# Key and value pooling and two engines' part of the weight conversion, emitted between a chunk's logarithm and its last three steps

## The chip, the cores and the metric

The kernel runs on one core of one Trainium2 chip. The metric is the device time of one execution in microseconds. Five queues run beside each other on the core: TensorE (PE, with its weight loads as PEld), VectorE (DVE), ScalarE (ACT), GpSimd (POOL) and SyncE (SP), which here issues every DMA.

## The reference

Three layers in a row: attention over pooled keys and values, a feed-forward layer with a rational activation, and a gated layer. The five weight matrices are float64, which the kernel reads as pairs of int32; the other inputs are float32.

```python
k_p = k.reshape(B, H, Sp, 8, D).mean(axis=3)      # B 8, H 8, S 576, D 64
v_p = v.reshape(B, H, Sp, 8, D).mean(axis=3)
scores = 1 / sqrt(D) * q @ k_p.transpose(0, 1, 3, 2)
attn = softmax(scores)
x = (attn @ v_p)                                  # 4608 tokens x 512
h = x @ w_in                                      # 512 x 2048
P = a[0] + a[1]*h + a[2]*h**2 + a[3]*h**3
Q = 1 + abs(b[0])*abs(h) + abs(b[1])*h**2
x = (P / (Q + 1e-6)) @ w_out                      # 2048 x 512
out = (sigmoid(x @ w_gate) * (x @ w_val)) @ w_out2
```

## The kernel before

**Chunks.** The feed-forward layer goes over 9 blocks of 512 tokens and, in each, over 16 slices of 128 hidden features: 144 chunks, counted by `n`. For each chunk the loop (L753 to L787) emits: `g1`, 12 matmuls into one of four PSUM banks tagged "h"; attention pieces for TensorE; `rational1` (three activations L509 to L511 on ScalarE, then L512 to L514 on VectorE, the polynomials); attention pieces that go first; `split_g` of the chunk before (L494 on ScalarE, L497 on GpSimd); `rational2` (the logarithm L520 and the exponential L522, which make the reciprocal in the chunk's own PSUM bank); `rational3` (L526 to L528 on VectorE); `g2` of the chunk three back, 12 matmuls into four accumulators; then the other attention pieces, and weights. Every engine works its queue in the order of emission.

**Attention.** A tile of up to 128 tokens goes through `scores` (matmuls L343; maximum and subtraction L354, L356 on VectorE), `exponential` (L362), `normalise` (L369 to L372 on VectorE, L373 on GpSimd), `a_transpose` and `attend`, whose end is L404 and L405. For each of 8 batches, five pieces of the keys are pooled by VectorE (L302) and five of the values by GpSimd (L319, L320). All are Python generators. A table `plan` gives each its step and a rank; `run(on_pe, n, part)` resumes each generator of the chunk once, for what it does on TensorE, and `run(off_pe, n, part)` resumes it a second time, for the rest. Part 0 goes ahead of `split_g`, part 1 behind `g2`. Pooling and its like have nothing on TensorE: `ew` (L408) yields at the first resumption and works at the second. The order of `plan` within a step also sets the order in which the pieces are loaded, three ahead.

**Weights.** A float64 matrix arrives as pairs of int32. `conv1` makes one float32 of each pair: L90 and L92 on ScalarE, L94 (a shift) and L96 (a mask and an or) on VectorE, L98 (an addition) on GpSimd. `conv2` splits it into a high and a low part: L102 on ScalarE, L103 on GpSimd. In chunks 0 to 15, `weights_a` converts a slice of `w_in` and one of `w_out` at each chunk's end, `conv1` two chunks ahead of `conv2`. From chunk 16 to chunk 111, `background` prepares the gated layer's weights in 12 units of 8 chunks: three loads, `conv1` at chunks 2, 3 and 6 of a unit, four subtractions L199 on GpSimd at chunk 4, splits by `bg_split` (L175 on ScalarE, L176 on GpSimd, a store L177 from one of two buffers) at chunks 5 to 7, and `conv2` at chunk 7 into the buffer whose store was issued at chunk 6.

Behind the chunks comes the gated layer, which TensorE fills.

Of the kernel before, what the change touches and what calls it, by code (L numbers as in the profile page):

```python
# [11 lines left out]
I32 = mybir.dt.int32  # L12
# [23 lines left out]
def attention_moe_glu_kernel(ctx: ExitStack, tc: tile.TileContext, q, k, v, w_in, w_out, ca, cb, w_gate, w_val, w_out2, out):  # L36
# [14 lines left out]
    NCH = (H * SP + P - 1) // P  # L51
# [24 lines left out]
    def new_tmp(name, tag="m", bufs=3):  # L76
        return rot.tile([P, 512], F32, tag=tag, name=name, bufs=bufs)
# [3 lines left out]

    def conv1(*raws):

        ws = [(raw[:, :, 1], raw[:, :, 0], new_tmp("wx").bitcast(I32)[:, :raw.shape[1]]) for raw in raws]
        for hw, lw, x in ws:


            nc.scalar.activation(hw.bitcast(F32), hw.bitcast(F32), AF.Copy, scale=2.0 ** -112)  # L90

            nc.scalar.activation(lw, lw.bitcast(U32), AF.Copy, scale=2.0 ** -29)  # L92
        for hw, lw, x in ws:
            nc.vector.tensor_scalar(out=x, in0=hw, scalar1=3, scalar2=None, op0=ALU.logical_shift_left)  # L94
        for hw, lw, x in ws:
            nc.vector.scalar_tensor_tensor(out=hw, in0=hw, scalar=-2 ** 31, in1=x, op0=ALU.bitwise_and, op1=ALU.bitwise_or)  # L96
        for hw, lw, x in ws:
            nc.gpsimd.tensor_tensor(out=hw, in0=hw, in1=lw, op=ALU.add)  # L98

    def conv2(raw, wh, wl, eng=nc.gpsimd):  # L100
        t = raw[:, :, 1].bitcast(F32)
        nc.scalar.activation(wh, t, AF.Copy)  # L102
        eng.tensor_tensor(out=wl, in0=t, in1=wh.bitcast(F32), op=ALU.subtract)  # L103
# [27 lines left out]
    def wi_conv1(f):  # L131
        conv1(wi_raw[f])
# [81 lines left out]
    with tc.manual_schedule():  # L214
# [29 lines left out]
        units, raws, loaded = [], {}, [0]  # L244
# [12 lines left out]
        def load_unit(start=False, tag=None):  # L257
            if loaded[0] == len(units):
                return
            u = units[loaded[0]]  # L260
            loaded[0] += 1
            if tag:
                t = tag[0].tile([P, 4 * P], F32, tag=tag[1], name="raw1")
            elif start:
                t = early([P, 4 * P], "raw0")
            else:
                t = raw_p.tile([P, 4 * P], F32, tag="raw", name="raw")
            if u[0] == "q":
                b, t0, n = tiles[u[1]]
                o = (b * S + t0) * H * D  # L270
                nc.sync.dma_start(t[:, :NJ * n], q[o:o + n * H * D].rearrange("(p x) -> p x", p=P))
            elif u[0] == "k":
                cols = k_cols(u[2])
                nc.sync.dma_start(t[:, :(cols.stop - cols.start) * POOL], k[u[1], :, cols.start * POOL:cols.stop * POOL])
            else:
                rows = v[u[1]].rearrange("h (s j) d -> (h s) (j d)", j=POOL)
                c = u[2]
                m = P if c < NCH - 1 else CL
                nc.sync.dma_start(t[:m], rows[c * P:c * P + m])
            raws[u] = t  # L280
            if not start and not tag:
                in_ring.add(u)
# [142 lines left out]
        plan = []  # L425
        n0 = len(of_block[0])

        def put(step, rank, pe, rest, gen, *a, use=()):
            plan.append((step, rank, len(plan), pe, rest, gen(*a), use))
# [17 lines left out]
        for b in range(1, B):  # L447
            e0, e1 = max(at[first[b - 1]], -2), at[last[b - 1]]
            for c in range(2 * NCH):
                w, f = (("k", pool_k), ("v", pool_v))[c // NCH]  # L450
                put(e0 + c * (e1 - 3 - e0) // (2 * NCH), 6, 1, 1, ew, f, b, c % NCH, use=[(w, b, c % NCH)])
            put(e1 - 2, 3.5, 1, 1, ew, place_k, b)
            put(e1 + (e1 > NF1), 1, 0, 0, ew, mask_v, b)
        plan.sort(key=lambda x: (x[0], x[4], x[1], x[2]))
        units += [u for x in plan for u in x[6]]
        lead = plan[0][0]
        on_pe, off_pe = {}, {}
# [4 lines left out]
        def run(which, step, part):  # L462
            for gen in which.get((step, part), []):
                next(gen, None)
# [37 lines left out]
        def g1(n):  # L502
            i, f = divmod(n, NF1)
            ys[n] = hidden(wi[f], xs[i])

        def rational1(n):
            h = ys[n]
            s, u, y = new_tmp("s", "su", 3), new_tmp("u", "su", 3), new_tmp("y", "y", 3)
            nc.scalar.activation(s, h, AF.Square)  # L509
            nc.scalar.activation(u, h, AF.Abs, scale=coef[:, 4:5])  # L510
            nc.scalar.activation(y, h, AF.Identity, scale=coef[:, 3:4], bias=coef[:, 2:3])  # L511
            nc.vector.scalar_tensor_tensor(out=u, in0=s, scalar=coef[:, 5:6], in1=u, op0=ALU.mult, op1=ALU.add)  # L512
            nc.vector.tensor_tensor(out=y, in0=h, in1=y, op=ALU.mult)
            nc.vector.scalar_tensor_tensor(out=y, in0=y, scalar=coef[:, 1:2], in1=h, op0=ALU.add, op1=ALU.mult)  # L514
            ys[n] = (h, s, u, y)

        def rational2(n):

            h, s, u, y = ys[n]
            nc.scalar.activation(s, u, AF.Ln, scale=2.0 ** LSH, bias=ONE * 2.0 ** LSH)  # L520

            nc.scalar.activation(h, s, AF.Exp, scale=-1.0, bias=LSH * math.log(2.0))  # L522

        def rational3(n):
            r, s, u, y = ys[n]
            nc.vector.scalar_tensor_tensor(out=u, in0=u, scalar=ONE, in1=r, op0=ALU.add, op1=ALU.mult)  # L526
            nc.vector.scalar_tensor_tensor(out=y, in0=y, scalar=coef[:, 0:1], in1=r, op0=ALU.add, op1=ALU.mult)  # L527
            nc.vector.scalar_tensor_tensor(out=y, in0=u, scalar=-2.0, in1=y, op0=ALU.add, op1=ALU.mult)  # L528

        def split_g(n):  # L530
            y = ys.pop(n)[3]
            gs[n] = g = g_p.tile([P, 2, TB], F32R, tag="g", name="g")
            split_hi(g, y)
            split_lo(g, y, nc.gpsimd)

        def g2(n):
            i, f = divmod(n, NF1)
            if f == 0:
                new_acc(i)
            g, wt = gs.pop(n), wo[f]  # L540
            for e in range(NJ):
                es = slice(e * P, (e + 1) * P)
                mm3(acc[i][e], wt[:, 1, es], wt[:, 0, es], g[:, 1], g[:, 0], f == 0, f == NF1 - 1)

        def g2_out(n):
            i, f = divmod(n, NF1)
            if f == NF1 - 1:
                for e in range(NJ):
                    store(acc[i][e], x2d[i][:, e], e < 2, *(("su", 3) if e == NJ - 1 else ()))
# [182 lines left out]
        def weights_a(p):  # L732

            for ahead, f, n in ((3, wi_conv2, NF1), (0, wo_conv2, NF1), (5, wi_conv1, NF1), (2, wo_conv1, NF1),
                                (8, wi_load, NF1), (5, wo_load, NF1)):
                if 0 <= p + ahead < n:
                    f(p + ahead)

        for st in range(lead, 0):
            run(on_pe, st, 0)  # L740
            run(on_pe, st, 1)
            run(off_pe, st, 0)
            run(off_pe, st, 1)
            if st == lead + 1:

                for x in range(NCH):
                    load_unit(tag=later[4 + x])
            weights_a(st)

        nc.scalar.activation(coef[:, 0:4], pc[:, 0:4], AF.Copy, scale=-1.0)  # L750
        nc.scalar.activation(coef[:, 4:6], pc[:, 4:6], AF.Abs)

        for n in range(N1):  # L753
            m = n - LAG
            if n == N1 - NF1:
                att.close()
                late = ctx.enter_context(tc.tile_pool(name="late", bufs=1))
            g1(n)
            run(on_pe, n, 0)
            rational1(n)  # L760
            run(off_pe, n, 0)
            if n >= 1:
                split_g(n - 1)
            rational2(n)
            rational3(n)
            if m >= 0:
                g2(m)
                g2_out(m)
            run(on_pe, n, 1)
            run(off_pe, n, 1)  # L770
            if n < NF1:
                weights_a(n)
            elif n % NF1 >= FS:
                wo_stream(n % NF1)
            background(n - NF1)
            x = n - (N1 - NF1)
            if x == 0:
                rawx = [xs_p.tile([P, 8 * TB], F32, tag="xs", name="rawx")]
                x_load(0)
            if 1 <= x <= NQ:  # L780
                ring_load(x - 1)
            if 3 <= x <= 6:
                x_prep(x - 3)
            if x in (4, 5):
                wo2_load(NF1 - NQ + x - 4)
            if x >= 7:
                wo2_load(x - 7)  # L787
# [68 lines left out]
```

## Time and profile before

| | |
|---|---|
| time, median of 3 runs | 1920.32 us (1919.8 to 1921.81) |
| the profiled execution | 1921.36 us, of which the span is 1919.5 us |
| TensorE busy | 1810.9 us, 94% |
| VectorE busy | 1223.6 us, 64% |
| ScalarE busy | 939.7 us, 49% |
| GpSimd busy | 899.5 us, 47% |
| chain that ended last | TensorE 58%, VectorE 24%, ScalarE 8%, issue 6%, DMA 2%, GpSimd 2% |

Busy shares are means over stages with different limits, so they are read by stretch. A group of instructions is named by its line in the kernel. Of an instruction the timeline gives the start, the time it took, and in brackets how long its engine had stood idle before it and what ended that. An instruction that stands still after it has been started, because something it needs on the way is taken, shows as one that takes longer, and not as a wait.

### The profile page before, as it was taken

What the parts mean: (1) busy time and instruction counts of PE and PEld (TensorE: products, weight loads), DVE (VectorE), ACT (ScalarE), POOL (GpSimd) and SP (SyncE); (2) the same over time, 40 slices, a digit from 0 to 9 for tenths busy, and PEclk for the clock granted to TensorE, in tenths of its full rate; (3) what the DMA queues carried; (4) which work ended last, traced back from release to release, by engine and by line L of the source; (5) the groups of instructions that cost most, each with busy time, mean ns of one, the idle gap of its engine ahead of it and who ended that gap; (6) DMA issues with size and microseconds to landing.
All of it is one profiled execution on the core that took longest, in us unless ns stands there. A gap on an engine that the chain in (4) does not pass through costs nothing.

```text
span 1919.5 us, 25166 instructions
## 1 busy us (share of the span) xinstructions
PE 1810.9 (94%) x8936; PEld 1565.9 (82%) x8936; DVE 1223.6 (64%) x1847; ACT 939.7 (49%) x1754; POOL 899.5 (47%) x855
## 2 busy tenths in 40 slices
PE   5588999999999999999999999999999999999999
PEld 4366777787777778777887899899999998998997
DVE  7999888889888888888778634334243333333331
ACT  4677767677666676766666522322222222222221
POOL 6668556665564665654224233424334335225231
PEclk9788999999999999999999999999999999999999
DMA  6343355344453444353135566465474573663661
GB/s 244 129 151 110 113 183 188 109 179 149 166 175 137 171 148 166 123 193 136 44 118 196 192 225 198 137 216 174 145 239 143 176 231 121 207 213 124 203 198 44
DMA packets 123118, 312.56 MB, mean 163 GB/s; under 512 B 11505, under 2 KB 43249, under 8 KB 122993
## 3 DMA queue, kind: packets, MB, share of 16 engines
q1 hardware_dynamic: 122992, 310.95, 48.1%
q8 instruction: 71, 1.16, 0.2%
q14 instruction: 55, 0.44, 0.1%
HBM read 257.95 MB, written 52.95 MB: 162 GB/s over the span
## 4 chain that ended last, share of the span: by engine, by line
PE 58%; DVE 24%; ACT 8%; issue 6%; DMA 2%; POOL 2%; SPq 0%; ACTq 0%; POOLq 0%; DVEq 0%
PE h L469 12%; PE h L471 11%; PE h L470 11%; DVE u L512 3%; DVE y L514 3%; DVE y L528 3%; DVE u L526 3%; DVE y L527 3%; ACT h L522 3%; PE accA L706 3%; PE accA L707 3%; PE h L707 3%; PE accA L705 3%; PE h L706 3%; PE h L705 3%
## 5 line engine op out<-in xcount | busy, mean ns | idle before, releaser
L642 DVE TENSOR_TENSOR t<-h,t 128x384 f32<-128x384 f32 x360 | 200.7, 558 | 388.3 <-ACT t L650 278.8
L695 POOL TENSOR_TENSOR t<-t 128x384 f32<-128x384 f32 x72 | 84.4, 1172 | 450.3 <-issue 255.0
L497 POOL TENSOR_TENSOR g<-y,g 128x512 fp32r<-128x512 f32 x144 | 189.1, 1313 | 207.5 <-ACT g L494 172.3
L469 PE MATMUL h<-xs,wi 128*128 128x512 f32 x576 | 234.3, 407 | 11.8 <-DVE xs L405 4.5
L469 PE MATMUL acc<-g,wo 128*128 128x512 f32 x576 | 233.1, 405 | 2.2 <-ACT g L494 2.2
L471 PE MATMUL h<-xs,wi 128*128 128x512 f32 x576 | 229.3, 398 | 3.0 <-DVE xs L405 3.0
L470 PE MATMUL h<-xs,wi 128*128 128x512 f32 x576 | 229.4, 398 | 0.0
L471 PE MATMUL acc<-g,wo 128*128 128x512 f32 x576 | 226.4, 393 | 2.4 <-POOL g L497 2.4
L470 PE MATMUL acc<-g,wo 128*128 128x512 f32 x576 | 225.4, 391 | 0.0
L471 PE MATMUL h<-xS,wq 128*128 128x384 f32 x576 | 193.0, 335 | 0.0
L469 PE MATMUL h<-xS,wq 128*128 128x384 f32 x576 | 192.8, 335 | 0.0
L470 PE MATMUL h<-xS,wq 128*128 128x384 f32 x576 | 192.7, 335 | 0.0
L512 DVE SCALAR_TENSOR_TENSOR u<-s,coef,u 128x512 f32<-128x512 f32 x144 | 133.9, 930 | 41.1 <-ACT u L510 40.8
L526 DVE SCALAR_TENSOR_TENSOR u<-u,h 128x512 f32<-128x512 f32 x144 | 99.0, 688 | 92.4 <-ACT h L522 90.6
L469 PE MATMUL h<-xA,wq 128*128 128x384 f32 x432 | 149.2, 345 | 0.0
L471 PE MATMUL h<-xA,wq 128*128 128x384 f32 x432 | 144.7, 335 | 0.0
L470 PE MATMUL h<-xA,wq 128*128 128x384 f32 x432 | 144.6, 335 | 0.0
L469 PEld LDWEIGHTS h<-xs,wi 128*128 128x128 f32 x576 | 111.1, 193 | 39.3 <-DVE xs L405 6.0
L528 DVE SCALAR_TENSOR_TENSOR y<-u,y 128x512 f32<-128x512 f32 x144 | 131.6, 914 | 4.9
L471 PEld LDWEIGHTS h<-xs,wi 128*128 128x128 f32 x576 | 111.2, 193 | 27.9 <-DVE xs L405 3.5
L520 ACT ACTIVATE s<-u 128x512 f32<-128x512 f32 x144 | 91.0, 632 | 87.6 <-DVE u L512 86.1
L469 PEld LDWEIGHTS acc<-g,wo 128*128 128x128 f32 x576 | 108.8, 189 | 28.1 <-ACT g L494 2.6
(122 smaller groups left out, 4290.9 us busy)
## 6 DMA issues: line engine op xcount, KB each, us to landing
wq<-w2d SPq DMA_DIRECT2D x252, 512.0 KB, 4.3
wo<-wod SPq DMA_DIRECT2D x88, 512.0 KB, 4.0
w2d<-wq SPq DMA_DIRECT2D x36, 512.0 KB, 2.9
x2d<-o SPq DMA_DIRECT2D x36, 256.0 KB, 2.3
out_dram<-o SPq DMA_DIRECT2D x36, 256.0 KB, 2.0
raw<-in_k_dram SPq DMA_DIRECT2D x32, 256.0 KB, 2.7
raw<-in_q_dram SPq DMA_DIRECT2D x32, 256.0 KB, 2.7
raw<-in_v_dram SPq DMA_DIRECT2D x32, 256.0 KB, 2.7
```

What stands on the lines that cost most here:

```text
L469: nc.tensor.matmul(out_, wl, xh, start=start, stop=False, skip_group_check=on)
L470: nc.tensor.matmul(out_, wh, xh, start=False, stop=False, skip_group_check=on)
L471: nc.tensor.matmul(out_, wh, xl, start=False, stop=stop, skip_group_check=on)
L497: eng.tensor_tensor(out=g[:, 1], in0=y, in1=g[:, 0].bitcast(F32), op=ALU.subtract)
L512: nc.vector.scalar_tensor_tensor(out=u, in0=s, scalar=coef[:, 5:6], in1=u, op0=ALU.mult, op1=ALU.add)
L520: nc.scalar.activation(s, u, AF.Ln, scale=2.0 ** LSH, bias=ONE * 2.0 ** LSH)
L526: nc.vector.scalar_tensor_tensor(out=u, in0=u, scalar=ONE, in1=r, op0=ALU.add, op1=ALU.mult)
L528: nc.vector.scalar_tensor_tensor(out=y, in0=u, scalar=-2.0, in1=y, op0=ALU.add, op1=ALU.mult)
L642: nc.vector.tensor_tensor(out=out_, in0=a, in1=b, op=ALU.add)
L705: nc.tensor.matmul(a[t], gh, wt[:, 0], start=(f == 0), stop=False)
L706: nc.tensor.matmul(a[t], gh, wt[:, 1], start=False, stop=False)
L707: nc.tensor.matmul(a[t], gl, wt[:, 0], start=False, stop=(f == NF2 - 1))
```

## The change

`conv1` is cut in two. Its activations (`conv1a`) stay where `conv1` was; its VectorE and GpSimd part (`conv1b`) is kept in a list and emitted by `gap()`, between `rational2` and `rational3` of the next chunk. For the pooling pieces the table's entry for the second resumption becomes part 2, which is run in the same place; the entry for the first stays part 1. In `plan`, they are sorted ahead of the other pieces of a step.

```diff
+    def conv1b(*raws):
         ws = [(raw[:, :, 1], raw[:, :, 0], new_tmp("wx").bitcast(I32)[:, :raw.shape[1]]) for raw in raws]
...
+    between = []
+
+    def conv1(*raws):
+        conv1a(*raws)
+        between.append(lambda: conv1b(*raws))
+
+    def gap():
+        for f in between:
+            f()
+        between.clear()
...
-                put(e0 + c * (e1 - 3 - e0) // (2 * NCH), 6, 1, 1, ew, f, b, c % NCH, use=[(w, b, c % NCH)])
+                st = e0 + c * (e1 - 3 - e0) // (2 * NCH)
+                put(st, 6, 1, 1 if st < 0 else 2, ew, f, b, c % NCH, use=[(w, b, c % NCH)])
...
-        plan.sort(key=lambda x: (x[0], x[4], x[1], x[2]))
+        plan.sort(key=lambda x: (x[0], (0, 2, 1)[x[4]], x[1], x[2]))
...
             weights_a(st)
+            gap()
...
             rational2(n)
+            run(off_pe, n, 2)
+            gap()
             rational3(n)
```

**VectorE, end of chunk 1 and start of chunk 2, before.** L94 and L96 are the conversion of a tile of `w_in` (`wiraw`) and one of `w_out` (`woraw`), L369 to L372 the normalisation of chunk 1.

```order
L514 SCALAR_TENSOR_TENSOR y<-y,coef,h 128x512
L526 SCALAR_TENSOR_TENSOR u<-u,h 128x512
L527 SCALAR_TENSOR_TENSOR y<-y,coef,h 128x512
L528 SCALAR_TENSOR_TENSOR y<-u,y 128x512
L369 TENSOR_REDUCE r<-e 64x8
L371 TENSOR_SCALAR r<-r 128x8
L372 RECIPROCAL r<-r 128x8
L94 TENSOR_SCALAR wx<-wiraw 128x512
L96 SCALAR_TENSOR_TENSOR wiraw<-wiraw,wx 128x512
L94 TENSOR_SCALAR wx<-woraw 128x512
L96 SCALAR_TENSOR_TENSOR woraw<-woraw,wx 128x512
L512 SCALAR_TENSOR_TENSOR u<-s,coef,u 128x512
```

And of the change, the same place; L98 and L100 are now the conversion's two lines, L528 to L530 the first three steps, L542 to L544 the last three, L384 to L387 the normalisation.

```order
L530 SCALAR_TENSOR_TENSOR y<-y,coef,h 128x512
L98 TENSOR_SCALAR wx<-wiraw 128x512
L100 SCALAR_TENSOR_TENSOR wiraw<-wiraw,wx 128x512
L98 TENSOR_SCALAR wx<-woraw 128x512
L100 SCALAR_TENSOR_TENSOR woraw<-woraw,wx 128x512
L542 SCALAR_TENSOR_TENSOR u<-u,h 128x512
L543 SCALAR_TENSOR_TENSOR y<-y,coef,h 128x512
L544 SCALAR_TENSOR_TENSOR y<-u,y 128x512
L384 TENSOR_REDUCE r<-e 64x8
L386 TENSOR_SCALAR r<-r 128x8
L387 RECIPROCAL r<-r 128x8
L528 SCALAR_TENSOR_TENSOR u<-s,coef,u 128x512
```

The conversion of chunk 0's tiles, emitted in chunk 0 before, stands in chunk 1 now, between the chunk's first three steps and its last three; chunk 1's own follows in chunk 2.

**GpSimd, chunks 21 to 23 (5 to 7 of a unit), before.** L497 is a chunk's low part, L373 a tile's normalisation, L98 the end of `conv1`, L176 and L103 low parts of split weights.

```order
L497 TENSOR_TENSOR g<-y,g 128x512
L373 TENSOR_TENSOR e<-e,r 128x576
L98 TENSOR_TENSOR wqraw<-wqraw 128x512
L176 TENSOR_TENSOR wq<-wqraw,wq 128x256
L176 TENSOR_TENSOR wq<-wqt,wq 128x256
L497 TENSOR_TENSOR g<-y,g 128x512
L176 TENSOR_TENSOR wq<-wqraw,wq 128x256
L103 TENSOR_TENSOR wq<-wqraw,wq 128x512
```

And of the change, where L513, L388, L102, L191 and L118 are the same in that order.

```order
L513 TENSOR_TENSOR g<-y,g 128x512
L388 TENSOR_TENSOR e<-e,r 128x576
L191 TENSOR_TENSOR wq<-wqraw,wq 128x256
L191 TENSOR_TENSOR wq<-wqt,wq 128x256
L513 TENSOR_TENSOR g<-y,g 128x512
L102 TENSOR_TENSOR wqraw<-wqraw 128x512
L191 TENSOR_TENSOR wq<-wqraw,wq 128x256
L118 TENSOR_TENSOR wq<-wqraw,wq 128x512
```

The end of `conv1` goes behind two splits and the next chunk's low part.

**VectorE, the end of chunk 7, before.** L302 is a pooled piece of the keys, L354 and L356 the softmax's maximum and subtraction.

```order
L528 SCALAR_TENSOR_TENSOR y<-u,y 128x512
L354 TENSOR_REDUCE mx<-sc 128x4 x2
L356 TENSOR_TENSOR e<-sc,mx 128x288 x2
L302 TENSOR_REDUCE kp<-raw 128x64
L94 TENSOR_SCALAR wx<-wiraw 128x512
```

And of the change, where L544, L317, L369 and L371 are the same.

```order
L544 SCALAR_TENSOR_TENSOR y<-u,y 128x512
L317 TENSOR_REDUCE kp<-raw 128x64
L369 TENSOR_REDUCE mx<-sc 128x4 x2
L371 TENSOR_TENSOR e<-sc,mx 128x288 x2
```

The piece stays behind the chunk's last step, and goes ahead of the softmax.

## Rows read from the trace of the kernel before

**Rows 1.** Busy time by stretch (chunks 0 to 15, 16 to 111): stretch, its length, engines.
```profile
core 0: us, PE busy (x) PEld busy (x) DVE busy (x) ACT busy (x) POOL busy (x), PEclk, DMA share, GB/s
45.90:208.70 162.80, 118.16 (x521) 95.04 (x518) 149.52 (x199) 110.94 (x202) 116.22 (x104) 0.84 0.37 127
208.70:886.10 677.40, 642.70 (x3085) 523.96 (x3086) 581.76 (x902) 467.32 (x875) 398.22 (x410) 0.99 0.45 157
```

**Rows 2.** Waits of VectorE, 46 to 209 us: total, times, longest.
```profile
DVE u L526 <- ACT h L522: 10.6, 14, 1.0
```

**Rows 3.** Waits of VectorE and of ScalarE, 209 to 886 us.
```profile
DVE u L526 <- ACT h L522: 57.8, 84, 1.0
...
ACT wq L102 <- DMA w2d<-wq: 29.3, 12, 3.3
```

**Rows 4.** Timeline of VectorE, chunks 1 and 2: start, time, instruction, [idle before].
```profile
60.67 0.74 DVE L512 SCALAR_TENSOR_TENSOR u<-s,coef,u 128x512 f32<-128x512 f32 x1
...
63.82 0.69 DVE L526 SCALAR_TENSOR_TENSOR u<-u,h 128x512 f32<-128x512 f32 x1 [1.03 <-ACT h L522]
...
66.90 0.39 DVE L94 TENSOR_SCALAR wx<-wiraw 128x512 int32<-128x512 int32 x1
67.32 4.03 DVE L96 SCALAR_TENSOR_TENSOR wiraw<-wiraw,wx 128x512 int32<-128x512 int32 x1
...
77.28 1.48 DVE L528 SCALAR_TENSOR_TENSOR y<-u,y 128x512 f32<-128x512 f32 x1
...
80.14 0.40 DVE L94 TENSOR_SCALAR wx<-wiraw 128x512 int32<-128x512 int32 x1
...
82.98 0.74 DVE L512 SCALAR_TENSOR_TENSOR u<-s,coef,u 128x512 f32<-128x512 f32 x1
```

**Rows 5.** Timeline of GpSimd, the same chunks.
```profile
67.06 1.23 POOL L373 TENSOR_TENSOR e<-e,r 64x576 f32<-64x576 f32 x1 [3.52 <-DVE r L372]
...
69.51 1.29 POOL L103 TENSOR_TENSOR wo<-woraw,wo 128x512 fp32r<-128x512 f32 x1
...
78.17 1.76 POOL L103 TENSOR_TENSOR wo<-woraw,wo 128x512 fp32r<-128x512 f32 x1
```

**Rows 6.** Group of the large key pieces, 0 to 900 us: busy us, mean ns.
```profile
L302 DVE TENSOR_REDUCE kp<-raw 128x64 f32<-128x512 f32 x32 | 21.0, 668 | 3.2 <-DMA raw<-in_k_dram 3.2
```

**Rows 7.** Timeline of ScalarE, chunk 2.
```profile
75.27 0.60 ACT L522 ACTIVATE h<-s 128x512 f32<-128x512 f32 x1 [0.81 <-DVE y L514]
```

**Rows 8.** Timelines of VectorE and of GpSimd, end of chunk 13.
```profile
192.33 1.52 DVE L94 TENSOR_SCALAR wx<-woraw 128x512 int32<-128x512 int32 x1
...
194.91 0.95 DVE L512 SCALAR_TENSOR_TENSOR u<-s,coef,u 128x512 f32<-128x512 f32 x1
...
191.82 1.74 POOL L497 TENSOR_TENSOR g<-y,g 128x512 fp32r<-128x512 f32 x1
```

**Rows 9.** Timelines and, with the DMA, the chain that ended last, chunks 22 and 23.
```profile
255.38 0.69 DVE L96 SCALAR_TENSOR_TENSOR wqraw<-wqraw,wx 128x512 int32<-128x512 int32 x1
...
263.48 0.83 DVE L512 SCALAR_TENSOR_TENSOR u<-s,coef,u 128x512 f32<-128x512 f32 x1 [1.96 <-ACT u L510]
...
256.20 1.43 POOL L98 TENSOR_TENSOR wqraw<-wqraw 128x512 int32<-128x512 int32 x1 [1.14 <-ACT u L510]
...
258.99 1.30 POOL L497 TENSOR_TENSOR g<-y,g 128x512 fp32r<-128x512 f32 x1
...
259.06 2.57 DMA w2d<-wq
...
261.71 0.66 ACT L102 ACTIVATE wq<-wqraw 128x512 fp32r<-128x512 f32 x1 [2.55 <-DMA w2d<-wq]
```

**Rows 10.** Line L199 (shortest, median, longest in ns) and two `L512` on VectorE's timeline.
```profile
L199 POOL TENSOR_TENSOR wqt<-wqraw x24: 840/1292/1368, 237.8 to 862.7; 128x256 f32<-128x256 f32 x24
L199 POOL TENSOR_TENSOR wqt<-wqraw,wqt x24: 729/750/1203, 238.8 to 864.0; 128x256 f32<-128x256 f32 x24
...
295.09 1.34 DVE L512 SCALAR_TENSOR_TENSOR u<-s,coef,u 128x512 f32<-128x512 f32 x1
...
356.81 4.93 DVE L512 SCALAR_TENSOR_TENSOR u<-s,coef,u 128x512 f32<-128x512 f32 x1 [0.87 <-ACT u L510]
```

More of the change, by code (lines that the diff above doesn't have):

```diff
@@ L79, in attention_moe_glu_kernel, with conv1a @@
     x2d = [dram.tile([P, NJ, TB], F32, name=f"x2d{i}", tag=f"x2d{i}") for i in range(NB)]
-    def conv1(*raws):
-        ws = [(raw[:, :, 1], raw[:, :, 0], new_tmp("wx").bitcast(I32)[:, :raw.shape[1]]) for raw in raws]
-        for hw, lw, x in ws:
+    def conv1a(*raws):
+        for raw in raws:
+            hw, lw = raw[:, :, 1], raw[:, :, 0]
             nc.scalar.activation(hw.bitcast(F32), hw.bitcast(F32), AF.Copy, scale=2.0 ** -112)
             nc.scalar.activation(lw, lw.bitcast(U32), AF.Copy, scale=2.0 ** -29)
+    def conv1b(*raws):
+        ws = [(raw[:, :, 1], raw[:, :, 0], new_tmp("wx").bitcast(I32)[:, :raw.shape[1]]) for raw in raws]
         for hw, lw, x in ws:
```

## The prediction

> **What bounds the kernel now.** I read the stretches first [rows 1]. From the first `L512` of the chunks (45.9 us) to that of chunk 16 VectorE is busy 149.5 of 162.8 us and TensorE 118.2, at a granted clock of 0.84: ten us a chunk, VectorE's. From chunk 16 to chunk 111 TensorE is busy 642.7 of 677.4 us and VectorE 581.8: TensorE is nearly full there, and whatever VectorE gains, no more than 677.4 - 642.7 = 34.7 us can come out of that stretch. Behind chunk 111 the change moves nothing.
>
> The waits come next. VectorE stands before `L526` for ScalarE's exponential: 10.6 us in 14 waits in the first stretch [rows 2], 57.8 in 84 in the second [rows 3], mostly 0.7 us a chunk. That is the hole into which the change puts work. In the second stretch ScalarE waits 29.3 us, 12 times, before `L102` for a store of converted weights [rows 3].
>
> The timelines show a second cost, which is no wait in any list: VectorE's conversion steps and `L528` and `L512` have two SBUF inputs or run in 0.4 us, and they stand still while GpSimd works. `L96` takes 0.69 us alone, and 4.03 in chunk 1 [rows 4], where it begins 0.26 us after GpSimd's `L373` and ends only after two `L103` behind it, at 70.80 [rows 5]. Elsewhere VectorE is let in between two GpSimd instructions: `L528` at 77.28 takes 1.48 us [rows 4] and pushes the second `L103` to 1.76 [rows 5].
>
> **What the change does.** By the printed order, TensorE's and ScalarE's queues stay as they are. On VectorE the pair `L94`, `L96` of a chunk's conversions goes from the end of chunk n to chunk n+1, between `L514` and `L526`. On GpSimd `L98` goes from ahead of `L497` of chunk n+1 to behind it. The pooling does not come to that place: its generator is resumed in the gap, where it reaches its `yield`, and does its work at the next resumption, behind the output matmuls as before, only now ahead of the softmax and not behind it. So the half of the title that speaks of pooling holds for no chunk, and I cost it as a swap of two neighbours: a key piece's 0.67 us ahead of the softmax's maximum and subtraction on VectorE, the value pooling ahead of `L373` on GpSimd. Nothing: a normalised tile is transposed a chunk later. Its bounds are no gain and the whole 21.0 us of the 32 large key pieces [rows 6], if each held the scores' banks where TensorE waits for them. On SP the same loads are issued, key or value piece ahead of the query tile of the same chunk; three buffers stay in rotation, and TensorE shows no wait for a query load, so nothing here either.
>
> **First stretch, chunks 1 to 10.** I walk the pair 1 and 2, which took 82.98 - 60.67 = 22.3 us [rows 4]; chunk 1 has a normalisation, chunk 2 a tile of scores, and five such pairs follow each other. Times from chunk 1's `L512`: its three steps end at 2.1 (`L526` begins at 63.82 after a wait of 1.03). The conversion (2.84, as at 80.14 to 82.98, the wait of the second `L96` included) fills the exponential's wait and ends at 4.9; the three last steps and the normalisation take 3.1 (63.82 to 66.90), to 8.0, say 8.2 because GpSimd's second `L98` is just ending at `L528`. Now GpSimd starts `L373` and two `L103`, 67.06 to 70.80 or 3.74 us [rows 5], and behind them, new in this place, `L497`, 1.3 [rows 9]: busy to between 12.0 and 13.3. Chunk 2's three steps end at 10.3 and its conversion meets that chain: it waits 0.5 us if let in at the next boundary, 3.0 if not. I take 2.5, since the 4.03 us row is the nearest. Conversion to 15.6, `L526` and `L527` to 17.0. Then a new collision: `L528` meets `L98` with two `L103` ready behind it, and before it met only the `L103`. Between 0.2 and 2.6 us; I take 1.05, let in at one boundary, as at 77.28. With `L528` and the scores 20.2, say 20.5. The pair gains 1.8 us, five pairs 9. The ends: 22.5 us with both waits whole (slower by 0.2), and 18.0. Lower it can't go: from `L522` of chunk 2 [rows 7] the transposed tile, scores, hidden matmuls and ScalarE's first steps lead to the next `L512`, 7.7 us later (75.27 to 82.98), and those are not moved.
>
> **Chunks 11 to 13** convert one tile each, which in chunk 13 takes 194.91 - 192.33 = 2.6 us because it stands against `L497` [rows 8]. In the gap `L497` is over and it takes 1.1; the exponential's 0.7 goes too; `L528` then pays for one GpSimd instruction, 0.8 as at 77.28. About 1.4 each, of which I count 1 because TensorE is nearly full by then. Together 3; the first stretch gains 12, between nothing and 26.
>
> **Chunks 16 to 111**, in twelve units of eight. Chunks 2, 3 and 6 of a unit convert, so the gaps of chunks 3, 4 and 7 are filled. Chunks 22 and 23 show what is worth most [rows 9]: on GpSimd two `L176` stood behind `L98`, which waited for `L96` of 255.38. So the store of their pieces set off at 259.06 and took 2.57 us, and `L102`, with the next chunk behind it on ScalarE, started at 261.71; VectorE's `L512` waited 1.96. Now the two `L176` stand ahead of `L98`, some 2.5 us sooner, and the store lands by about 259.2. `L102` then waits for the conversion in chunk 23's gap: `L512` begins at 256.0 and `L514` ends 2.1 later, at 258.1; `L94` and `L96` end at 259.2, `L98` (1.43 at 256.20, part of it waiting) at 260.4. It starts 1.3 us sooner. Twelve times that is 15.6; the ends are nothing, if ScalarE is late for another reason, and the whole 29.3 of the list [rows 3].
>
> The gaps of chunks 3 and 4 of a unit fill 0.73 each, 1.5. But in chunk 4 `L98` now has the four `L199` right behind it (1.29 and 0.75 us in turn [rows 10]), some 4.1 us that start as VectorE comes to `L526`; `L528` and the next `L512` then each wait for one of them, 0.8, as `L512` at 295.09 did (1.34 for 0.74 [rows 10]). I set the two against each other: nothing. Of 15.6 us I count 9, since TensorE, 95% busy, can turn only part into time.
>
> The sum: -12 - 9 = -21 us from the profiled 1921.36, which lies 1 us over the median 1920.32: **1900 us**.
>
> **A rule against the trace.** The row of 4.03 us shows VectorE kept out for three GpSimd instructions [rows 4, 5]. The Trainium skill (SBUF — State Buffer, the section on two separate sides) says that the port pair shared by VectorE and GpSimd is an exclusive lock, held by whichever instruction starts first for the whole of that one instruction. By it a blocked step would wait for the rest of one instruction only. The trace agrees at 77.28 and not at 67.32, and I keep to the rows.
>
> **The rivals.**
> - *Larger gain.* VectorE is let in at every boundary: the pairs take 18.0 (5 x 4.3 = 21, and 5 for chunks 11 to 13), and the unit's saving comes out nearly whole, 18: -44, 1877 us. For it speak the rows at 77.28 and 295.09, against it that at 67.32. This is the time by the skill's rule above.
> - *No change.* VectorE's gain becomes waiting: in the even chunks for the 7.7 us path through TensorE [rows 7], after chunk 16 for TensorE [rows 1]. Within 4 us of now, 1919. Against it: the odd chunks have no such path.
> - *Slower.* In chunk 4 of each unit VectorE is kept out for the whole chain of `L199`, as `L512` was for 4.93 us at 356.81 [rows 10]. `L528` is due 1.4 us after the conversion, `L98` ends at 1.2 and the four `L199` at 5.3, so it starts 3.9 us late instead of 0.8, and twelve times 3.1 is 37: 1937 us. It decides from 21 / 12 = 1.75 us more in each unit than I allow. Against it speaks 295.09, where VectorE came in between two `L199`.
>
> **Numbers.** A change under 0.2% (3.8 us) can't be told from none. Forecast 0.55 (its own range 1888 to 1912), larger gain 0.20, no change 0.13, slower 0.12. Faster: 0.55 + 0.20 less a sliver, 0.75; same 0.13; slower 0.12. The range leaves out the far part of the two outer cases: 1874 to 1921.
>
> **What would show it.** Right: the waits before `L526` in the first stretch fall from 10.6 to about 2 us, and from 57.8 to about 33 in the second (36 of the 84 filled); chunks 1 to 10 take some 102 us (five pairs of 20.5) instead of 111; `L102` waits for the store or `L98` 1.3 us less each time. Wrong: `L528` in chunks 1 to 10 at 3 us, `L528` or `L512` beside `L199` at over 2, or TensorE's idle time from chunk 16 on unchanged near 35 us.

## The result, and the profile after

| | before | after |
|---|---|---|
| time, median (lowest to highest) of 4 runs | 1920.53 us (1919.8 to 1921.81) | 1896.54 us (1894.58 to 1897.76) |
| ratio, 95% interval | 1 | 0.9873 (0.9856 to 0.9891) |
| the profiled execution | 1921.36 us | 1894.58 us |
| first `L512` (now `L528`) of chunk 0 to that of chunk 16 | 162.8 us | 158.4 us |
| chunk 16 to chunk 112 | 677.4 us | 656.8 us |
| chunk 112 to chunk 143 | 190.9 us | 190.6 us |
| busy: TensorE, VectorE | 1810.9, 1223.6 us | 1804.6, 1242.5 us |
| chain that ended last | TensorE 58%, VectorE 24%, ScalarE 8% | TensorE 67%, VectorE 21%, ScalarE 4% |

The kernel became 24 us faster, where 21 were forecast. The split was forecast as 12 and 9; by the two profiles it came out as 4.4 and 20.6. In the changed kernel `L528` to `L530` are a chunk's first three steps on VectorE and `L542` to `L544` its last three; `L98`, `L100` and `L102` are the conversion's shift, mask and addition; `L388` is the normalisation on GpSimd, `L513` a chunk's low part, `L190` and `L191` the splits, `L117` and `L118` `conv2`, `L214` the four subtractions.

The same two stretches of the profile after, by busy time (stretch, length, engines):

```profile
core 0: us, PE busy (x) PEld busy (x) DVE busy (x) ACT busy (x) POOL busy (x), PEclk, DMA share, GB/s
45.90:204.20 158.30, 118.62 (x516) 95.40 (x514) 154.43 (x198) 112.60 (x200) 115.36 (x104) 0.87 0.38 131
204.20:861.10 656.90, 636.14 (x3083) 521.24 (x3082) 597.09 (x903) 469.29 (x875) 393.79 (x407) 1.00 0.46 162
```

Against [rows 1], TensorE's idle time in the second stretch fell from 34.7 to 656.90 - 636.14 = 20.8 us; the other 6.6 us left its busy time, at a granted clock of 1.00 for 0.99. VectorE is busy for 15.3 us more there. That is time in which it stands still: the work is the same.

The waits of VectorE from 46 to 200 us, then of VectorE and of ScalarE from 200 to 860 us (total, times, longest). The first stretch ends at 204.2 us, so chunk 15's wait of 0.7 us before `L542` stands in the second list:

```profile
DVE u L528 <- ACT u L526: 2.6, 1, 2.6
DVE u L542 <- ACT h L538: 0.7, 1, 0.7
```
```profile
DVE u L542 <- ACT h L538: 31.4, 48, 1.0
DVE u L528 <- ACT u L526: 17.3, 26, 1.4
...
ACT wq L117 <- POOL wqraw L102: 15.7, 8, 2.3
ACT wq L117 <- DMA w2d<-wq: 11.4, 4, 3.2
...
ACT wq L190 <- DMA w2d<-wq: 5.7, 4, 2.1
```

The holes are filled as forecast: with that wait counted in the first stretch, 10.6 [rows 2] became 1.5 us and 57.8 [rows 3] became 30.7. But `L117` still waits 27.1 us in its 12 times, where the 29.3 of [rows 3] stood: for the store in 4 of them and for the moved conversion in 8. The other wait for a store, at `L190`, fell to 5.7 us from the 13.5 of its line `L175` before:

```profile
ACT wq L175 <- DMA w2d<-wq: 13.5, 6, 3.7
```

Part of what was filled came back as stand-still. The groups of VectorE in the second stretch, after (busy us, mean ns):

```profile
L544 DVE SCALAR_TENSOR_TENSOR y<-u,y 128x512 f32<-128x512 f32 x96 | 93.1, 969 | 3.3
...
L98 DVE TENSOR_SCALAR wx<-wqraw 128x512 int32<-128x512 int32 x36 | 36.0, 1001 | 0.0
L100 DVE SCALAR_TENSOR_TENSOR wqraw<-wqraw,wx 128x512 int32<-128x512 int32 x36 | 25.5, 708 | 1.2
```

and before:

```profile
L528 DVE SCALAR_TENSOR_TENSOR y<-u,y 128x512 f32<-128x512 f32 x96 | 82.1, 855 | 3.3
...
L96 DVE SCALAR_TENSOR_TENSOR wqraw<-wqraw,wx 128x512 int32<-128x512 int32 x36 | 34.1, 947 | 1.2
L94 DVE TENSOR_SCALAR wx<-wqraw 128x512 int32<-128x512 int32 x36 | 18.6, 517 | 0.0
```

The shift takes 1001 ns instead of 517 and the chunk's last step 969 instead of 855, the mask 708 instead of 947: 36 x 0.484 + 96 x 0.114 - 36 x 0.239 = 19.8 us more in these three groups.

In the first stretch the same is to be seen one by one. Chunk 2 on VectorE's timeline after:

```profile
66.28 0.75 DVE L528 SCALAR_TENSOR_TENSOR u<-s,coef,u 128x512 f32<-128x512 f32 x1
...
68.33 3.75 DVE L98 TENSOR_SCALAR wx<-wiraw 128x512 int32<-128x512 int32 x1
...
75.88 1.62 DVE L544 SCALAR_TENSOR_TENSOR y<-u,y 128x512 f32<-128x512 f32 x1
```

and on GpSimd's:

```profile
66.33 1.70 POOL L388 TENSOR_TENSOR e<-e,r 64x576 f32<-64x576 f32 x1 [2.02 <-DVE r L387]
68.00 1.29 POOL L118 TENSOR_TENSOR wi<-wiraw,wi 128x512 fp32r<-128x512 f32 x1
69.26 1.29 POOL L118 TENSOR_TENSOR wo<-woraw,wo 128x512 fp32r<-128x512 f32 x1
70.51 1.28 POOL L513 TENSOR_TENSOR g<-y,g 128x512 fp32r<-128x512 f32 x1
```

The shift starts 0.33 us after the first `L118` and ends at 72.08, 0.29 behind the end of `L513`: it stood through three GpSimd instructions, 3.35 us longer than the 0.40 of [rows 4] (forecast: 2.5). `L544` takes 0.93 us longer than its 0.69 (forecast: 1.05).

### The profile page after: what moved, and what is told of

Same layout as the page of the kernel before. It is cut to its first block, busy times and chain, and to the rows that moved or that the text cites. A ratio compares the mean times of both kernels' runs of the same rounds, so it can differ in the third digit from the quotient of the medians.

```text
span 1892.7 us, 25138 instructions
## 1 busy us (share of the span) xinstructions
PE 1804.6 (95%) x8936; PEld 1564.4 (83%) x8936; DVE 1242.5 (66%) x1847; ACT 943.0 (50%) x1754; POOL 896.4 (47%) x855
## 4 chain that ended last, share of the span: by engine, by line
PE 67%; DVE 21%; ACT 4%; issue 4%; DMA 2%; POOL 2%; SPq 0%; ACTq 0%; POOLq 0%; DVEq 0%
PE h L485 13%; PE h L487 12%; PE h L486 12%; PE acc L485 3%; PE acc L487 3%; PE acc L486 3%; PE accA L722 3%; PE accA L723 3%; PE h L722 3%; PE h L723 3%; PE accA L721 3%; PE h L721 3%; DVE u L528 3%; PE psx L413 3%; DVE y L544 3%
## 5 line engine op out<-in xcount | busy, mean ns | idle before, releaser
L513 POOL TENSOR_TENSOR g<-y,g 128x512 fp32r<-128x512 f32 x144 | 190.6, 1324 | 245.7 <-ACT g L510 186.7
L528 DVE SCALAR_TENSOR_TENSOR u<-s,coef,u 128x512 f32<-128x512 f32 x144 | 132.1, 918 | 32.2 <-ACT u L526 31.9
L544 DVE SCALAR_TENSOR_TENSOR y<-u,y 128x512 f32<-128x512 f32 x144 | 143.9, 999 | 4.9
L525 ACT ACTIVATE s<-h 128x512 f32<-128x512 f32 x144 | 85.0, 590 | 110.4 <-PE h L487 110.3
L542 DVE SCALAR_TENSOR_TENSOR u<-u,h 128x512 f32<-128x512 f32 x144 | 98.5, 684 | 56.0 <-ACT h L538 54.3
```

Source lines behind the costliest of these rows:

```text
L513: eng.tensor_tensor(out=g[:, 1], in0=y, in1=g[:, 0].bitcast(F32), op=ALU.subtract)
```

## The experiments

Ratios are to the kernel before, run beside each of them, with a 95% interval. "The change" is the changed kernel.

**The two halves.** `conv1b` left in the gap, the pooling entries as before; and the pooling entries of the change, `conv1b` called at the end of its own chunk (`now=True` emits it at once).

```diff
 the change, conversion alone
-                put(st, 6, 1, 1 if st < 0 else 2, ew, f, b, c % NCH, use=[(w, b, c % NCH)])
+                put(st, 6, 1, 1, ew, f, b, c % NCH, use=[(w, b, c % NCH)])
...
-        plan.sort(key=lambda x: (x[0], (0, 2, 1)[x[4]], x[1], x[2]))
+        plan.sort(key=lambda x: (x[0], x[4], x[1], x[2]))
```

> The conversion's VectorE and GpSimd part in the gap as in the change; the pooling table and its sorting as before. If the swap of pooling and softmax is worth nothing, as the prediction has it: 1896 to 1898 us, as the change. If the pooling carries part of the gain: 1902 us or more; if the swap costs something, under 1893.

```diff
 the change, pooling alone: the same for all four calls
-        conv1(wi_raw[f])
+        conv1(wi_raw[f], now=True)
```

> The pooling pieces sorted ahead of the softmax and worked at the first resumption behind the output matmuls, as in the change; the conversion at the end of its own chunk as before. If the swap is worth nothing: 1918 to 1923 us. If it carries part of the gain: 1915 or less.

Measured: the conversion alone 0.9942 (0.9927 to 0.9956), 11 us of 1921.85; the pooling alone 0.9955 (0.9943 to 0.9967), 8.6 us. The pooling swap, which the prediction held at nothing, is nearly as large as the rest. By its profile the gain lies in the second stretch alone: 666.4 us instead of 677.4, while the first took 164.8 instead of 162.8. The two together make 19.7 us of the change's 24.4 (by its ratio).

**The conversion's two stretches.** Only `background`'s conversions in the gap, then only those of `weights_a`; pooling as before.

```diff
 the conversion alone, second stretch
-        conv1(wi_raw[f])
+        conv1(wi_raw[f], now=True)
...
-        conv1(wo_raw[f])
+        conv1(wo_raw[f], now=True)
```

> Only the 36 conversions from chunk 16 on go into the gap; those of chunks 0 to 13 and the pooling stay as before. By the trace of the change (20.5 us gained from chunk 16 to 111): 1899 to 1902 us, and 162.8 us for chunks 0 to 15. By the prediction's split (9 of 21 us there): 1910 to 1912.

```diff
 the conversion alone, first stretch
-            conv1(bg["raw"][r - 2])
+            conv1(bg["raw"][r - 2], now=True)
...
-            conv1(bg["raw"][2])
+            conv1(bg["raw"][2], now=True)
```

> Only the conversions of chunks 0 to 13 go into the gap; the 36 later ones and the pooling stay as before. By the trace of the change (4.5 us gained in chunks 0 to 15): 1914 to 1917 us. By the prediction's split: 1907 to 1910. If the collisions of the conversion with GpSimd's chain eat the filled wait whole: 1919 to 1922.

Measured: 0.9967 (0.9956 to 0.9978), 6.3 us, and 0.9974 (0.9964 to 0.9985), 5.0 us. They add up to the 11 of the conversion alone. So the term of 12 is 5, and the term of 9 is 6. The first stretch came where the trace of the change had put it; the second, at 1914.2 us, gained less than either expectation. (Its profile is of its slowest execution, 1919.16 us, and nothing is read from it.)

**Which conversion of a unit.** Only the third (chunk 6 to the gap of chunk 7); only the first two; and, without touching VectorE's or ScalarE's order, the kernel before with the third's addition on GpSimd behind the two splits, so that the store sets off earlier.

```diff
 third alone, against the conversion alone in the second stretch
-            conv1(bg["raw"][r - 2])
+            conv1(bg["raw"][r - 2], now=True)
```

> Of the 36 conversions from chunk 16 on only the third of each unit (chunk 6 of the unit, ahead of which the two splits now stand on GpSimd) goes into the gap. Theory 1, the earlier store is what the second stretch gains: 1902 to 1906 us. Theory 2, the filled wait before the last three steps is what it gains, each of the three conversions alike: a third of 20 us, 1912 to 1915.

```diff
 first two alone, against the same
-            conv1(bg["raw"][2])
+            conv1(bg["raw"][2], now=True)
```

> Only the first two conversions of each unit go into the gap, which leaves the splits and their store as before. Theory 1 (the earlier store): 1918 to 1921 us. Theory 2 (the filled wait): two thirds of 20 us, 1905 to 1909.

```diff
 the kernel before, addition behind the splits
-            conv1(bg["raw"][2])
+            adds = conv1(bg["raw"][2], add=False)
...
+            adds()
```

> The kernel before with one piece of order changed: in chunk 6 of a unit GpSimd's addition, which ends the conversion, goes behind the two splits; VectorE's and ScalarE's queues are as before. Theory 1 (the earlier store): 1905 to 1912 us, and the waits of ScalarE before the last split of a unit fall from 29 us to under 15. Theory 2 (the filled wait): 1917 to 1921, whatever those waits do.

Measured: the third 0.9968 (0.9955 to 0.998), 6 us; the first two 0.9983 (0.9974 to 0.9992), 3.3 us; the addition behind the splits 0.9969 (0.9958 to 0.9979), 6 us. The first two, at 1916.3 us, lie between what the two theories gave, the addition behind the splits, at 1914.2, between them too; so neither theory is the whole. The third and the first two make 9.4 us where all three together gave 6.3, which the intervals allow. ScalarE's waits from 208 to 878 us, in the kernel before:

```profile
ACT wq L102 <- DMA w2d<-wq: 26.1, 11, 2.9
```

with the addition behind the splits (`L106` is its `L102`):

```profile
ACT wq L179 <- DMA w2d<-wq: 13.6, 5, 4.0
ACT wq L106 <- DMA w2d<-wq: 5.9, 6, 1.9
...
ACT wq L106 <- POOL wq L180: 1.1, 1, 1.1
```

and with the third conversion in the gap (`L120`):

```profile
ACT wq L120 <- POOL wqraw L102: 20.4, 11, 2.3
...
ACT wq L120 <- DMA w2d<-wq: 3.1, 1, 3.1
```

An earlier store alone takes the wait from 26.1 us in that window to 7.0, and 6 us of the time with it: about a third. The third conversion in the gap gives as much, but not by that wait. There it is still 23.5 us, now for the addition, which comes late from the gap; what shrinks is VectorE's wait for the exponential, in the chunks where the hole is filled (before, then with the third conversion in the gap):

```profile
DVE u L526 <- ACT h L522: 57.1, 83, 1.0
```
```profile
DVE u L545 <- ACT h L541: 49.3, 72, 1.6
```

That the 6 us come from there is read from these waits; no run parts it from the splits that now stand ahead of the addition. The filled holes of the first two, which the prediction set at nothing against the collisions with `L214`, are worth 3.3.

**Keys or values.** Of the pooling swap, only the value pieces (GpSimd) go ahead of the softmax and the normalisation; only the key pieces (VectorE). The conversions are where they were.

```diff
 pooling alone, values ahead; for the keys, w == "v"
-                put(st, 6, 1, 1 if st < 0 else 2, ew, f, b, c % NCH, use=[(w, b, c % NCH)])
+                put(st, 6, 1, 1 if st < 0 or w == "k" else 2, ew, f, b, c % NCH, use=[(w, b, c % NCH)])
```

> Of the pooling swap alone only the value pieces go ahead of the softmax; key pieces and conversions as before. Theory G, GpSimd pools while it would wait for the normalisation, and its later splits and stores come sooner: most of the 9 us of the swap, 1912 to 1915 us. Theories S and V (below) give a third or less: 1917 to 1920.

> Of the pooling swap alone only the key pieces go ahead of the softmax; value pieces and conversions as before. Theory V, VectorE's order is what gains, a buffer of keys comes free 1.5 us sooner, and with it what stands behind its reload on SP: most of the 9 us, 1912 to 1915. Theory G: 1918 to 1921.

Measured: values 0.9944 (0.993 to 0.9958), 10.8 us; keys 0.9999 (0.999 to 1.0008), nothing. The swap's whole gain comes with the value pieces, which GpSimd pools (the 10.8 us and the 8.6 of the whole swap have overlapping intervals). Chunk 101 shows how. GpSimd before (`L319`, `L320` pool values, `L176` are the splits for the store):

```profile
806.62 1.30 POOL L497 TENSOR_TENSOR g<-y,g 128x512 fp32r<-128x512 f32 x1
810.72 1.15 POOL L373 TENSOR_TENSOR e<-e,r 128x576 f32<-128x576 f32 x1 [2.80 <-DVE r L372]
811.83 1.72 POOL L319 TENSOR_TENSOR raw<-raw 64x256 f32<-64x256 f32 x2
813.62 0.32 POOL L320 TENSOR_TENSOR vp<-raw 64x64 f32<-64x64 f32 x1
813.90 0.73 POOL L176 TENSOR_TENSOR wq<-wqt,wq 128x256 fp32r<-128x256 f32 x1
```

and with the values ahead (`L337`, `L338`, `L391`, `L194`):

```profile
799.90 1.29 POOL L516 TENSOR_TENSOR g<-y,g 128x512 fp32r<-128x512 f32 x1
801.15 1.27 POOL L337 TENSOR_TENSOR raw<-raw 64x256 f32<-64x256 f32 x2
802.50 0.65 POOL L338 TENSOR_TENSOR vp<-raw 64x64 f32<-64x64 f32 x1
804.15 1.15 POOL L391 TENSOR_TENSOR e<-e,r 128x576 f32<-128x576 f32 x1 [1.01 <-DVE r L390]
805.26 1.19 POOL L194 TENSOR_TENSOR wq<-wqt,wq 128x256 fp32r<-128x256 f32 x1
```

Before, GpSimd stood 2.80 us at the normalisation, with the pooling ready behind it; then the pooling stood ahead of the splits, which began 3.18 us after the normalisation. Now the pooling fills that wait and the splits begin 1.11 us after it. The queue behind follows. ScalarE in chunk 102, before, and with the values ahead:

```profile
819.41 0.43 ACT L175 ACTIVATE wq<-wqraw 128x256 fp32r<-128x256 f32 x1 [3.74 <-DMA w2d<-wq]
```
```profile
809.85 0.45 ACT L193 ACTIVATE wq<-wqraw 128x256 fp32r<-128x256 f32 x1 [0.75 <-POOL g L516]
```

On VectorE chunk 102 takes, from its first step to that of the next, 821.24 - 811.46 = 9.78 us before, and 811.69 - 804.74 = 6.95 us with the values ahead.

The loads on SP have a part in this. SP before, and with the values ahead (`L271` and `L289` load a query tile, `L156` and `L174` output weights, `L177` and `L195` are the stores):

```profile
813.97 0.33 SPq L271 DMA_DIRECT2D raw<-in_q_dram  x1
814.35 0.42 SPq L156 DMA_DIRECT2D wo<-wod  x1
815.38 1.71 SPq L177 DMA_DIRECT2D w2d<-wq  x2
```
```profile
803.17 0.33 SPq L289 DMA_DIRECT2D raw<-in_q_dram  x1
803.55 0.42 SPq L174 DMA_DIRECT2D wo<-wod  x1
807.18 1.72 SPq L195 DMA_DIRECT2D w2d<-wq  x2
```

In both, the first store sets off as soon as its second split ends. But before, the pooling frees a buffer at 813.94, the loads that waited for it go out 1.4 us ahead of the store, and the store takes 4.0 us from issue to landing; with the values ahead they go out 4.0 us ahead of it, and it takes 2.6. How much of the 10.8 us is GpSimd's order and how much such loads, no run parts. Over the stretch GpSimd's wait at the normalisation shrinks, before and with the values ahead:

```profile
POOL e L373 <- DVE r L372: 82.0, 27, 4.3
```
```profile
POOL e L391 <- DVE r L390: 66.6, 26, 4.3
```

**The other suspect for the stores, SP's queue.** In the kernel before, loads that refill the pooling buffers are issued behind all stores of the chunk.

```diff
-                load_unit()
+                owed[0] += 1
...
+            loads()
```

> The kernel before, with the loads that refill attention buffers issued on SP at the end of the chunk, behind its stores of converted weights and its stream of the output weights; no compute instruction is moved. Theory S, the swap gains because a store no longer stands on SP behind a load that waits for a buffer: 1911 to 1915 us, and ScalarE's waits for stores from chunk 16 on fall from 43 to under 30 us. Theories G and V: 1918 to 1922, or slower if the later loads are waited for.

Measured: 0.9973 (0.9963 to 0.9983), 5.2 us. From 208 to 878 us, ScalarE's 13.5 us of waiting for stores at `L175` are gone, while `L102` waits longer than the 26.1 us there before:

```profile
ACT wq L102 <- DMA w2d<-wq: 31.0, 11, 3.5
```

So the loads ahead of the stores cost something in the kernel before. Two things changed with them, which this run doesn't part: 12 of the 48 stores had set off more than 0.1 us after their split, 10.1 us in all, and now none does; and a store took 3.6 us in the mean from issue to landing, and now 2.8. The time, 1915.11 us, is at the edge of what theory S gave, and ScalarE's waits for stores, 31.0 us here, did not fall under its 30.

**What the title says, and all of it together.** The pooling really emitted in the gap (its first resumption ahead of it), in the changed kernel; then that with the loads last.

```diff
-                put(st, 6, 1, 1 if st < 0 else 2, ew, f, b, c % NCH, use=[(w, b, c % NCH)])
+                put(st, 6, 1 if st < 0 else 0, 1 if st < 0 else 2, ew, f, b, c % NCH, use=[(w, b, c % NCH)])
```

> The change, with the pooling pieces from chunk 0 on resumed one part earlier, so that they are really worked between the logarithm and the last three steps. If the wait before those steps is worth filling wherever it stands (31 us of it are left, 48 times, and 27 key pieces of 0.67 us fall into this stretch): 1885 to 1892 us. If the value pooling, which then runs on GpSimd under the last of the three steps, keeps VectorE out for as long: 1895 to 1903.

> The change with the pooling really in the gap (as in e8_pooling_in_the_gap) and the loads issued last (as in e11_loads_last). If the loads' 5 us come on top: 1887 to 1890 us. If the order of GpSimd already lets the stores set off early enough, or TensorE, busy for all but some 15 us from chunk 16 on, takes no more: 1892 to 1896.

Measured: 0.986 (0.9845 to 0.9875), 1893.94 us, the best version here, though its interval overlaps that of the change; with the loads last 0.9888 (0.9872 to 0.9905), 1899.54 us, no better. The former lies between its two ranges, the latter above both of its own. The loads' 5.2 us don't add to it. No run shows why; in the two profiles TensorE's idle time in the second stretch is nearly the same (653.5 - 633.0 = 20.5 us, and 662.9 - 641.1 = 21.8 with the loads last), and what differs is its busy time, at a granted clock of 1.00 and of 0.98.

## Why the prediction was right and wrong

**The total** is right, 1896.5 for 1900, and that is luck: both terms of its sum were too large (12 for 5.0, 9 for 6.3), and one that stood at nothing, worth 8.6, made up for them. Of its signs of being right the two waits came (1.5 us for 2, 30.7 for 33), the 102 us for chunks 1 to 10 and the 1.3 us less at `L102` did not; none of its signs of being wrong came.

- *The pooling swap: "Nothing"* failed; it measures 8.6 us as a whole and 10.8 for the values alone. The prediction looked at what the normalised tile is needed for, and not at what stands in GpSimd's queue behind it: the wait at `L373` had ready work behind it, and that work, with the loads that it released, then delayed splits, stores and ScalarE. The wait of 2.80 us and the pooling behind it stand in the trace of before. The reading of the code was right: the pooling doesn't come to the gap.
- *First stretch, "gains 12"* failed in size: 5.0 us alone, 4.4 in the change. The pair of chunks 1 and 2 takes 78.89 - 57.74 = 21.15 us, where 20.5 were forecast and 22.3 stood before; chunks 1 to 10 take 105.6 us instead of the 102 forecast (before 110.5). The mechanism is the one named (the conversion meets GpSimd's chain), its price 3.35 instead of 2.5. The term of 3 for chunks 11 to 13 had the wrong sign: chunk 0's conversion moves on (14.73 to 11.89 us), and the shift is paid back at the end, where chunks 11 to 14 take 34.9 us in all instead of 31.6.
- *Chunks 16 to 111, "I count 9"*: 6.3 us from the conversions, near in size, by another mix. `L102` starts no 1.3 us sooner; its waits stay at 27.1 us. The earlier store can be worth 6 us, as the addition behind the splits shows, but in the change the conversion takes its place ahead of `L117`. By the waits, what carries the term is the filled hole in chunk 7, and the 3.3 us in chunks 3 and 4 that had been set off against collisions. Those collisions cost less than was counted: 0.44 us at chunk 4's `L544` and nothing at the step behind it, for 0.8 at each.
- *The rival "Slower"* did not come. Beside the four `L214` VectorE got in between two, as the prediction expected: `L544` in chunk 4 of a unit takes 1.27 us in the mean of twelve, where 0.83 stood before. (The 4.93 us at 356.81 [rows 10], on which the rival leaned, stood beside `L373`, four `L176` and `L497`, and beside no `L199`.) In chunk 20:

```profile
233.42 1.31 DVE L544 SCALAR_TENSOR_TENSOR y<-u,y 128x512 f32<-128x512 f32 x1
```
```profile
232.21 1.04 POOL L102 TENSOR_TENSOR wqraw<-wqraw 128x512 int32<-128x512 int32 x1 [1.09 <-DVE wqraw L100]
233.33 0.85 POOL L214 TENSOR_TENSOR wqt<-wqraw 128x256 f32<-128x256 f32 x1
234.26 1.08 POOL L214 TENSOR_TENSOR wqt<-wqraw,wqt 128x256 f32<-128x256 f32 x1
```

- *The rival "Larger gain"* did not come: the time landed near the forecast and not at 1877, and the shift of chunk 2 was held through the rest of three instructions. The Trainium skill (SBUF — State Buffer, section on two separate sides) has the shared port pair held for the whole of the one instruction that starts first. The row above of chunk 20 agrees with that rule, that of chunk 2 does not.
- *The rival "No change"* did not come either: TensorE's idle time in the second stretch fell by 13.9 us.

**Open.** The two halves alone make 19.7 us, the change 24.4: the difference, 4.7 us, is within what the intervals leave (about 5), so whether they help each other isn't settled. What makes VectorE wait for one GpSimd instruction in one place and three in another was not tried in a run. The traces of before and after narrow it down. Counted from 30 to 900 us, for VectorE instructions that took at least 0.25 us too long: where GpSimd paused between two instructions, for some 0.08 us, VectorE got in at all 57 such places; where the next one followed without a pause, it got in at 89 and was passed over at 61. Nearly all of the pauses stand where an instruction reads what the one before it wrote, as between the first two `L214` of chunk 20 (234.18 to 234.26); beside the shift of chunk 2 there is none. What decides in the places without a pause stays open.

## What to carry to other kernels

Wherever an in-order queue waits, look at what stands ready behind the waiting instruction, on the side engines and on the queue that issues the DMAs too: moving ready work ahead of a wait on GpSimd was worth as much here (10.8 us) as filling VectorE's holes (11). When a hole is filled on VectorE, count the GpSimd chain that the moved instruction will meet, above all one of ready instructions that don't read each other's results, and what its own consumers now wait for. A chunk-wise shift of work isn't a saving at its two ends: what leaves the first chunk turns up after the last.

## What was not expected of the hardware

A plain shift of int32 on VectorE, 0.40 us alone, stood for 3.75 us through three back-to-back GpSimd instructions; steps of the kind of `L528` and `L544` still take 4.9 to 5.4 us in single places of the second stretch (chunks 38, 53 and 70):

```profile
348.23 5.38 DVE L528 SCALAR_TENSOR_TENSOR u<-s,coef,u 128x512 f32<-128x512 f32 x1 [0.42 <-ACT u L526]
```

against 0.69 to 0.75 where nothing holds them up. The longest is chunk 0's last step, 6.25 us beside five GpSimd instructions without a pause, before the change and after it. None of that is in a list of waits.
